# One transfer or four for the first K unit of a decode layer, and four transfers or one for a bias

## The chip, the cores and the metric

The kernel runs on one core of a Trainium2 chip, in one launch. The metric is the device time of that launch in microseconds. The time before is 134.47 us, the median of five runs that lie between 134.28 and 134.51 us.

## The reference

Two tokens (B = 2, one position each, D = 576) go through a layer norm, and then through two branches whose results are added to the input. Branch A is attention against a cache, over the last W = 2048 of 8192 positions; 32 query heads share 16 K/V heads of 128 numbers. Branch B is an MLP with a squared ReLU. Everything in memory is bf16.

```python
xn = layernorm(x)                                  # x: (2, 1, 576)
q  = (xn @ wq).reshape(2, 1, 32, 128)              # wq: (576, 4096)
k  = repeat(k_cache[:, :, 6144:8192, :], 2)        # k_cache, v_cache: (2, 16, 8192, 128)
v  = repeat(v_cache[:, :, 6144:8192, :], 2)
p  = softmax(q . k / sqrt(128))
a  = (p . v) @ wo                                  # wo: (4096, 576)
h  = relu(xn @ w1 + b1) ** 2                       # w1: (576, 4608)
out = x + a + h @ w2 + b2                          # w2: (4608, 576)
```

What has to be read is the last quarter of both caches (33.6 MB) and the four weight matrices (20.1 MB).

## The kernel before

The attention is cut into NU = 8 units. Unit u holds TH = 4 K/V heads of one of the two tokens: 4 x 2048 positions x 128 numbers, 2 MB of K and 2 MB of V. In the tile of a unit, partition p = 4 c + h holds 64 consecutive positions (chunk c of 32) of head h, that is one contiguous row of 16 KB. `unit_view` makes that view of the cache, `issue_kv` takes a buffer and returns the calls that load it, `load_k` and `load_v` call them. K and V units share a pool of six buffers (`kvpool`), which the second MLP matrix uses too at the end.

For each unit `transposes` turns K on TensorE into kT in PSUM (four 128x128 fp32 transposes for each of eight groups), ScalarE and VectorE copy kT to SBUF in turn, `scores` multiplies it with the queries, `softmax` follows, and two units later `pv` multiplies with V. The queries come from `q_block`, which runs after the transposes of unit 0 and needs wq in two transfers: `wq_rem` (0.5 MB) and `wq_big` (4 MB). The MLP's first matrix w1 comes behind the attention's K units, and then the second, w2, whose last rows end the kernel: mlp_o, one copy to `fin_sb` and one transfer out.

All large transfers are issued by SyncE (SP in the profile) in program order: K 0, wq_rem, wq_big, K 1, V 0, K 2, V 1, K 3, V 2, and so on. ScalarE issues the small ones: x at the very start (`xb_sb`, 2 rows), some rows of w2 in five transfers (`w2x_sb`: four of 5 rows of 9 KB, on every fourth partition, and one of 96 rows of 1 KB), the MLP's first bias b1 (`b1_sb`, 4 partitions of 2304 bytes) and the second bias b2 (into row 2 of `xb_sb`).

A planner fixes the order on each engine when the program is built, and places an instruction as early as its operands allow; so the small transfers of ScalarE do not stand where the source has them. It also gives each transfer, SP's and ScalarE's in one common order, one of eight completion semaphores in turn. A transfer that takes a semaphore again waits on its issuing engine until the previous transfer on that semaphore has landed. In the program before the common order begins: x (semaphore 0), K 0 (1), first w2x (2), wq_rem (3), wq_big (4), second w2x (5), b1 in four transfers (6, 7, 0, 1), b2 (2), K 1 (3), V 0 (4), K 2 (5), third w2x (6), V 1 (7), fourth w2x (0), K 3 (1), V 2 (2). So K 1 waits for wq_rem, V 0 for wq_big, K 2 for the second w2x, V 1 and K 3 for two of the b1 transfers, V 2 for b2 and for the buffer of K 0.

Of the kernel before, what the change touches and what calls it, by code (L numbers as in the profile page):

```python
# [9 lines left out]
BF16 = mybir.dt.bfloat16  # L10
# [6 lines left out]
def kernel(  # L17
# [14 lines left out]
    nc = tc.nc  # L32
    P = 128
# [10 lines left out]
    TH = 4  # L44
# [7 lines left out]
    UE = NJ * Dh  # L52
# [13 lines left out]
    NG4 = 4  # L66
# [28 lines left out]
    kvpool = ctx.enter_context(tc.tile_pool(name="kvpool", bufs=6))  # L95
# [17 lines left out]
    k_tiles, v_tiles, wq_tiles, w1_tiles, wo_tiles, w2_tiles = {}, {}, {}, {}, {}, {}  # L113
# [3 lines left out]
    def unit_view(cache, u):  # L117
        tq, b = divmod(u, B)
        return cache[b, tq * TH:(tq + 1) * TH, S0:Sk, :].rearrange("h (c j) d -> c h (j d)", c=CP)

    def issue_kv(tiles, cache, u, name, parts=1):
        tl = kvpool.tile([P, UE], BF16, tag="kv", name=f"{name}_{u}")
        v = unit_view(cache, u)
        n = UE // parts
        tiles[u] = tl
        return [lambda i=i: nc.sync.dma_start(out=tl[:, i * n:(i + 1) * n], in_=v[:, :, i * n:(i + 1) * n])
                for i in range(parts)]
# [62 lines left out]
    nc.vector.memset(eps_t[:], 1e-5)  # L190
    warm = const.tile([B, 2], F32, name="warm")
    nc.scalar.activation(out=warm[:, 0:1], in_=eps_t[:], func=ACT.Sqrt)
    for f in issue_kv(k_tiles, A_k_cache, 0, "k"):
        f()
    NW = 2
    for i in range(NW):
        issue_wq(i)
# [43 lines left out]
    for sg in range(S):  # L241
# [12 lines left out]
                          in_=own[:].unsqueeze(2).to_broadcast([P, NC, HQ // NC]))  # L254
# [275 lines left out]
    load_v(2)  # L530
    b1_sb = const.tile([NG4, HW], BF16, name="b1_sb")
    b1_rows = B_b1.rearrange("(g n) -> g n", g=NG4)
    for i in range(0, NG4, NG4 // 4):
        nc.scalar.dma_start(out=b1_sb[i:i + NG4 // 4, :], in_=b1_rows[i:i + NG4 // 4, :])
    sel4 = const.tile([NG4, P], BF16, name="sel4")
    nc.vector.tensor_copy(out=sel4[:].rearrange("p (g s) -> p g s", s=32),
                          in_=ident[0:NG4, 0:NG4].unsqueeze(2).to_broadcast([NG4, NG4, 32]))
# [67 lines left out]
```

## Time and profile before

| | before |
|---|---|
| median of five runs | 134.47 us |
| the profiled execution | 134.28 us |
| its span | 132.5 us |
| mean granted TensorE clock | 0.834 |
| bytes moved by DMA | 53.76 MB, mean 406 GB/s over the span |
| busy: PE, PEld, DVE, ACT, POOL | 65%, 40%, 43%, 35%, 4% of the span |
| K 0: issued, first transpose that reads it | 0.72 us, 8.45 us |
| wq_rem landed (K 1 is issued) | 9.71 us |
| wq_big landed (V 0 is issued, `q_block` starts) | 19.65 us |
| b1 and b2 issued by ScalarE | 14.40 to 15.82 us |
| last matmul of w2, last copy, transfer out issued | 129.36 us, 129.64 us, 129.95 us |

The span runs from the first to the last event of the profiled execution; the run's time is 1.78 us longer than the span. Busy shares are shares of the whole span, so an engine with 65% can still be the one that is waited for in one stage and idle in another. The DMA share of a stretch is the mean over 16 DMA engines of the time that their packets took; a packet counts where it starts, so a short stretch can show more than 1 and the next one less. In the page's list of DMA queues, q1 carries what SP issues and q10 what ScalarE issues.

### The profile page before, as it was taken

The numbers are of one execution on the slowest core, as the hardware profiler recorded it, in microseconds if no ns is written. First come the engines' busy times: TensorE is split into PE (matmuls) and PEld (weight loads), VectorE is DVE, ScalarE is ACT, GpSimd is POOL, SyncE is SP. The second block draws the span as 40 slices with busy tenths as digits, with TensorE's granted clock in tenths as the row PEclk, the third lists the DMA queues.
The fourth block names the chain that finished last, engine by engine and source line by source line (L and its number), as shares of the span: only waits on it lengthen the run. The fifth ranks groups of instructions, "written<-read, shape, count | busy, mean of one in ns | idle before, by whom it ended". The sixth has DMA issues, their size and how long they took to land.

```text
span 132.5 us, 2337 instructions
## 1 busy us (share of the span) xinstructions
PE 85.5 (65%) x982; PEld 53.0 (40%) x982; DVE 57.2 (43%) x156; ACT 46.6 (35%) x64; POOL 5.2 (4%) x17
## 2 busy tenths in 40 slices
PE   0069509599597679397399689778600938655941
PEld 0058403266364436264256346445400424404930
DVE  6724400525477466476336759456320043344000
ACT  5715500418773375176235346376100040000000
POOL 6000000010010000100100010010100000000000
PEclk9999955958999999999757999999995595555595
DMA  4999999999999999999999999999999999999960
GB/s 154 395 448 456 415 402 427 435 425 435 429 423 424 445 411 424 431 440 420 423 425 445 425 440 433 435 430 444 467 406 388 440 411 444 414 417 444 410 245 1
DMA packets 4219, 53.76 MB, mean 406 GB/s; under 512 B 503, under 2 KB 730, under 8 KB 1246
## 3 DMA queue, kind: packets, MB, share of 16 engines
q1 hardware_dynamic: 4032, 53.32, 94.7%
q10 hardware_dynamic: 178, 0.31, 0.6%
q8 instruction: 7, 0.11, 0.3%
q14 instruction: 2, 0.02, 0.0%
HBM read 53.62 MB, written 0.00 MB: 405 GB/s over the span
## 4 chain that ended last, share of the span: by engine, by line
DMA 61%; PE 6%; DVE 1%; ACT 1%; issue 1%; ACTq 0%
DMA v<-in_A_v_cache_dram 28%; DMA w<-in_B_w_dram 17%; DMA k<-in_A_k_cache_dram 16%; PE kT_ps L108 4%; PE o_ps L105 1%; ACT kT L325 1%; PE sc_ps L105 1%; ACT p L357 1%; DVE pT L360 1%; DVE kT L327 0%; DVE o L386 0%; ACT fin_sb L573 0%; PE out_ps L105 0%; DVE o L384 0%; PE op_ps L105 0%
## 5 line engine op out<-in xcount | busy, mean ns | idle before, releaser
L108 PE MATMUL kT_ps<-ident_f,k 128*128 128x128 f32 x256 | 41.2, 309 | 8.8 <-DMA k<-in_A_k_cache_dram 5.2
L108 PEld LDWEIGHTS kT_ps<-ident_f,k 128*128 128x128 f32 x256 | 32.3, 158 | 22.6 <-issue 10.4
L325 ACT COPY kT<-kT_ps 128x1024 bf16<-128x1024 bf16 x32 | 31.9, 1012 | 22.7 <-PE kT_ps L108 18.4
L327 DVE COPY kT<-kT_ps 128x1024 bf16<-128x1024 bf16 x32 | 21.8, 683 | 13.8 <-PE kT_ps L108 13.5
L105 PE MATMUL sc_ps<-kT,qz 128*32 128x512 bf16 x128 | 10.1, 398 | 6.4 <-DVE kT L327 5.0
L105 PE MATMUL o_ps<-v,pT 128*32 128x512 bf16 x128 | 12.1, 475 | 0.0
L357 ACT ACTIVATE p<-sc_ps,bias 128x512 bf16<-128x512 f32 x8 | 5.5, 688 | 17.6 <-DVE gown L353 17.6
L105 PEld LDWEIGHTS <-xnT 128*2 128x2 bf16 x100 | 3.1, 114 | 16.8 <-issue 16.5
L346 DVE TENSOR_REDUCE m<-sc_ps 128x1 f32<-128x512 f32 x8 | 5.5, 692 | 6.9 <-PE sc_ps L105 6.9
L386 DVE SCALAR_TENSOR_TENSOR o<-o_ps,in_s,o 128x128 f32<-128x128 f32 x24 | 8.3, 347 | 0.5
L360 DVE STREAM_TRANSPOSE pT<-p 128x512 bf16<-128x512 bf16 x8 | 5.7, 712 | 6.5 <-ACT p L357 6.5
L105 PE MATMUL h_ps<-w_big,xnT 128*2 128x384 bf16 x48 | 3.7, 492 | 7.2 <-DMA w_big<-in_B_w_dram 7.2
L573 ACT CAST fin_sb<-out_ps 113x144 bf16<-113x144 f32 x1 | 0.3, 279 | 21.7 <-PE out_ps L105 21.7
L105 PE MATMUL q_ps<-wq_big,xnT 128*2 128x512 bf16 x32 | 3.6, 626 | 4.7 <-DMA wq_big<-in_A_wq_dram 4.7
L350 POOL PARTITION_ALL_REDUCE gmax<-m x8 | 2.9, 365 | 89.4 <-DVE m L348 89.4
L384 DVE TENSOR_SCALAR o<-o_ps,in_s 128x128 f32<-128x128 f32 x8 | 2.7, 338 | 8.1 <-PE o_ps L105 8.1
L105 PEld LDWEIGHTS <-qz 128*32 128x32 bf16 x128 | 2.1, 94 | 10.0 <-DVE kT L327 7.5
L105 PE MATMUL op_ps<-o,of_h 128*128 128x129 f32 x16 | 4.0, 334 | 3.2 <-DVE o L386 3.2
L451 DVE TENSOR_TENSOR hrow<-t 98x384 bf16<-98x384 f32 x3 | 1.6, 556 | 10.0 <-ACT t L450 9.8
L105 PEld LDWEIGHTS <-hT_sb 128*17 128x17 bf16 (+2 forms) x172 | 4.3, 117 | 3.1 <-issue 3.1
L105 PE MATMUL out_ps<-w,hT_sb 128*17 128x144 bf16 x136 | 4.1, 279 | 2.0 <-DMA w<-in_B_w_dram 1.9
L450 ACT ACTIVATE t<-h_ps 98x384 f32<-98x384 f32 x3 | 1.4, 489 | 10.3 <-PE h_ps L105 10.0
(74 smaller groups left out, 52.9 us busy)
## 6 DMA issues: line engine op xcount, KB each, us to landing
k<-in_A_k_cache_dram SPq DMA_DIRECT2D x8, 2048.0 KB, 18.1
v<-in_A_v_cache_dram SPq DMA_DIRECT2D x8, 2048.0 KB, 9.9
wo<-in_A_wo_dram SPq DMA_DIRECT2D x2, 2304.0 KB, 27.4
w_big<-in_B_w_dram SPq DMA_DIRECT2D x1, 4608.0 KB
wq_big<-in_A_wq_dram SPq DMA_DIRECT2D x1, 4096.0 KB, 17.6
w<-in_B_w_dram SPq DMA_DIRECT2D x3, 1296.0 KB, 30.9
w_rem<-in_B_w_dram SPq DMA_DIRECT2D x1, 576.0 KB, 28.2
w<-in_B_w_dram SPq DMA_DIRECT2D x1, 576.0 KB, 22.1
```

What stands on the lines that cost most here:

```text
L105: tc.keep_in_program_order(nc.tensor.matmul(*a, **k))
L108: tc.keep_in_program_order(nc.tensor.transpose(*a, **k))
L325: nc.scalar.copy(out=kT, in_=kT_ps[:])
L327: nc.vector.tensor_copy(out=kT, in_=kT_ps[:])
L346: nc.vector.tensor_reduce(out=m1[:], in_=sc_ps[:], axis=AX.X, op=ALU.max)
L350: nc.gpsimd.partition_all_reduce(gmax[:], m2[:], channels=P, reduce_op=ReduceOp.max)
L357: nc.scalar.activation(out=p_sb[:], in_=sc_ps[:], func=ACT.Exp, bias=bias[:, 0:1], scale=scale, accum_out=o1[:, Dh:Dh + 1])
L360: nc.vector.transpose(out=pT[:].rearrange("p j r -> p (j r)"), in_=p_sb[:])
L384: nc.vector.tensor_scalar(scalar1=in_s[:, 0:1], scalar2=None, op0=ALU.mult, **kw)
L386: nc.vector.scalar_tensor_tensor(scalar=in_s[:, k:k + 1], in1=o1[:, 0:Dh], op0=ALU.mult, op1=ALU.add, **kw)
L450: nc.scalar.activation(out=t1, in_=mlp["ps"][k][0:RB, :], func=ACT.Relu)
L451: nc.vector.tensor_tensor(out=hrow[:, k * HB:(k + 1) * HB], in0=t1, in1=t1, op=ALU.mult)
```

## The change

Two places change. The first K unit is no longer loaded by one transfer of 128 rows of 16 KB, but by four of 32 rows, one for each head: transfer h fills partitions h, h + 4, h + 8, ..., h + 124. The bytes and where they lie in the end are the same. And the bias b1, which came in four transfers of one row, comes in one transfer of four rows.

```diff
-    for f in issue_kv(k_tiles, A_k_cache, 0, "k"):
-        f()
+    k_tiles[0] = kvpool.tile([P, UE], BF16, tag="kv", name="k_0")
+    for h in range(TH):
+        nc.sync.dma_start(out=k_tiles[0][h:P:TH, :], in_=unit_view(A_k_cache, 0)[:, h, :])
...
-    for i in range(0, NG4, NG4 // 4):
-        nc.scalar.dma_start(out=b1_sb[i:i + NG4 // 4, :], in_=b1_rows[i:i + NG4 // 4, :])
+    for i in range(0, NG4, NG4):
+        nc.scalar.dma_start(out=b1_sb[i:i + NG4, :], in_=b1_rows[i:i + NG4, :])
```

The number of transfers stays 40: three more on SP, three fewer on ScalarE. The common order begins differently, though, and with it who waits for whom: x (0), K 0 head 0 (1), first w2x (2), K 0 head 1 (3), second w2x (4), b1 (5), K 0 head 2 (6), b2 (7), K 0 head 3 (0), wq_rem (1), wq_big (2), and from K 1 (3) on as before. On SP, in the order of issue, the transfers now wait like this:

| transfer on SP | waits before for | waits after for |
|---|---|---|
| K 0 | nothing | heads 0 to 2: nothing; head 3: x |
| wq_rem | nothing | K 0 head 0 |
| wq_big | nothing | first w2x |
| K 1 | wq_rem | K 0 head 1 |
| V 0 | wq_big | second w2x |
| K 2 | second w2x | b1 |
| V 1 | second b1 row | b2 |
| K 3 | fourth b1 row | wq_rem |
| V 2 | b2, K 0 transposed | wq_big, K 0 transposed |

ScalarE issues b1 and b2 directly behind the second w2x transfer, before its first copy of kT; before, they stood behind its fourth copy. The first transpose of K 0 waits for four transfers. The order of all other instructions on TensorE, VectorE, ScalarE and GpSimd is unchanged.

## The prediction

> **What bounds the kernel now.** I read four views in this order: busy time by stage, the timeline of the first ten microseconds, SP's waits, and fine stretches around the first packets. The stage view has the length of a stretch, five engines' busy time, the TensorE clock, the DMA share and GB/s.
>
> ```profile
> 0.00:2.00 2.00, 0.00 (x0) 0.00 (x0) 1.07 (x9) 0.68 (x1) 1.47 (x8) 1.00 0.00 1
> 2.00:30.00 28.00, 15.86 (x112) 10.22 (x113) 10.12 (x34) 10.21 (x16) 1.20 (x3) 0.83 1.01 426
> 30.00:60.00 30.00, 23.38 (x221) 14.52 (x219) 18.38 (x43) 17.28 (x24) 1.10 (x3) 0.99 1.01 427
> 60.00:90.00 30.00, 23.53 (x201) 14.16 (x200) 17.49 (x43) 14.29 (x19) 1.09 (x3) 0.89 1.00 428
> 90.00:126.00 36.00, 21.06 (x388) 13.01 (x388) 10.19 (x30) 3.87 (x7) 0.36 (x1) 0.67 1.00 428
> 126.00:129.40 3.40, 1.52 (x64) 1.06 (x63) 0.00 (x0) 0.00 (x0) 0.00 (x0) 0.98 0.59 229
> ```
>
> From 2 to 126 us the DMA share is 1.00 at 426 to 428 GB/s in every stage, while no compute engine is full. So the DMA engines set the end: time is the moment when they start, plus bytes over rate, plus a fixed tail (last bytes of w2, 0.27 us of matmul, 0.28 us of copy, the transfer out). A change counts if it moves the start of the feed, lets the feed run dry, lowers its rate or adds packets. When a transfer is issued, or K 0 transposed, does not count while others are queued.
>
> The timeline (start, duration, what) shows how the feed begins.
>
> ```profile
> 0.72 0.61 SPq L126 DMA_DIRECT2D k<-in_A_k_cache_dram  x1
> 0.73 0.56 ACTq L188 DMA_DIRECT2D xb_sb<-in_A_x_dram  x1
> 1.39 0.57 SPq L138 DMA_DIRECT2D wq_rem<-in_A_wq_dram  x1
> 1.44 0.80 ACTq L184 DMA_DIRECT2D w2x_sb<-in_B_w_dram  x1
> 2.00 0.42 SPq L132 DMA_DIRECT2D wq_big<-in_A_wq_dram  x1
> 8.45 5.79 PE L108 MATMUL kT_ps<-ident_f,k 128*128 128x128 f32 x27 [1.32 <-DMA k<-in_A_k_cache_dram]
> 9.71 0.56 SPq L126 DMA_DIRECT2D k<-in_A_k_cache_dram  x1
> ```
>
> SP's waits show the semaphores at work: K 1 stands 7.3 us until wq_rem has landed, V 0 9.4 us until wq_big has.
>
> ```profile
> SPq L126 <- DMA wq_big<-in_A_wq_dram: 9.4, 1, 9.4
> SPq L126 <- DMA wq_rem<-in_A_wq_dram: 7.3, 1, 7.3
> ```
>
> Stretches of 0.1 us show when the first packets start: x at 1.6 to 1.7, K 0 from 2.1 on.
>
> ```profile
> 1.60:1.70 0.10, 0.00 (x0) 0.00 (x0) 0.10 (x2) 0.10 (x1) 0.10 (x2) 1.00 0.07 23
> 2.00:2.10 0.10, 0.00 (x0) 0.00 (x0) 0.10 (x1) 0.10 (x1) 0.10 (x1) 1.00 0.00 0
> 2.10:2.20 0.10, 0.00 (x0) 0.00 (x0) 0.10 (x1) 0.10 (x1) 0.10 (x2) 1.00 4.92 1311
> 2.20:2.30 0.10, 0.00 (x0) 0.00 (x0) 0.10 (x2) 0.10 (x1) 0.10 (x1) 1.00 1.71 492
> 2.30:2.40 0.10, 0.00 (x0) 0.00 (x0) 0.10 (x2) 0.10 (x1) 0.10 (x1) 1.00 2.25 655
> 2.40:2.50 0.10, 0.00 (x0) 0.00 (x0) 0.09 (x2) 0.10 (x1) 0.10 (x1) 1.00 0.57 164
> ```
>
> **Part 1, the feed starts earlier.** A row of 16 KB starting within 0.1 us counts as 164 GB/s, so 8, 3, 4 and 1 packets start in the last four stretches, one for each DMA engine, at 2.24 us in the mean: 1.52 us after the issue at 0.72. x, with 2 rows, needed 0.92 us (0.73 to 1.65). A quarter has 32 rows. If it took as long as 128 rows nothing is gained; if as long as 2 rows, 0.60 us. A straight line between the two rows gives 0.92 + 0.60 x 30/126 = 1.06 us, a gain of 0.46. SP's issue itself hardly follows the rows (w2x of 96 rows took 0.32 us, one row of b1 0.25), so I take a little less: -0.40 us, bounds 0 and -0.60.
>
> **Part 2, three more transfers.** Each adds a completion on up to 16 engines, 48 small packets. q10's 178 packets take 0.6% of 16 x 132.5 us, 12.7 us; its 0.31 MB take 11.7 us at the 26.6 GB/s per engine of q1 (53.32 MB in 94.7%). The rest is 6 ns a packet: 48 x 6 ns / 16 = +0.02 us, bounds 0 and 0.05.
>
> Whether a transfer of its own has a fixed cost that the queue doesn't hide shows in wq_rem: 0.52 MB behind K 0, it landed 9.71 - 8.45 = 1.26 us after it, which is 416 GB/s and leaves no room for one. [...]
>
> **Part 3, new waits on SP.** Behind each stands every later transfer on SP.
> - Head 3 waits for x, which VectorE reads at 2.93. First bytes by 2.93 + 1.52 = 4.45; heads 0 to 2 (1.57 MB at 426 GB/s, 3.7 us from 1.84) last to 5.5. Nothing.
> - wq_rem waits for head 0: 1.84 + 1.23 us of bytes + 0.4 (the first packets are slow: all 16 of them start before 2.5, none between 2.5 and 3.0) + 0.4 to the landing = 3.9, first bytes 5.4; K 0 lasts to 7.2. Nothing.
> - wq_big waits for the first w2x. Before, its five rows start between 5.5 and 6.5, behind K 0's first rows, and its five completions between 6.5 and 7.5, so it landed near 7.5. wq_rem's bytes ran out on the engines between 8.5 and 9.3, say 8.9; with Part 1, 8.5. If w2x moves with the feed it lands at 7.1 and wq_big's bytes come at 8.6, 0.1 late; if it is served sooner, since fewer rows stand ahead of it, nothing is late; if it stays at 7.5, 0.5 is lost. I take +0.05, bounds 0 and 0.5; the rival below goes further.
> - K 1, V 0, K 2, V 1, K 3 and V 2 wait for small or earlier transfers. They were issued from 9.71 to 24.13 behind wq_big's 9.9 us of bytes with the share at 1.01; earlier issue gains nothing, and the later order of waits is unchanged.
>
> **Part 4, b1 and ScalarE.** Three issues of 0.24 to 0.26 us leave ScalarE at 14.4 to 15.8, where it idles 8.6 us until 24.03: 0. b1 and b2 are now issued near 5.3, ahead of its first copy at 9.60, in its 3.68 us of idle time; without that cover they would delay kT copies by 0.5 us, and PE waits until 19.67 for wq_big anyway. Bytes of b1 stay equal; should one engine have carried all four rows and end last, 6.9 KB / 26.6 GB/s = 0.26 us go. No row shows that; I take 0.
>
> **Part 5, TensorE.** The first transpose waits for four landings instead of one. They come by about 8.1; the work behind it has 4.7 us of slack before wq_big. 0.
>
> **Sum.** -0.40 + 0.02 + 0.05 = -0.33 us. The profiled run took 134.28 us (span 132.5, 1.78 around it), 0.19 under the median; its span would be 132.17. Against the median: 134.47 - 0.33 = **134.14 us**.
>
> **Rivals.**
> - *The start doesn't move*, or the new wait gives it back: 134.47 + 0.02, and 134.4 to 134.6 with half the bounds. For it: SP's issue does not shrink with rows (0.33 to 0.61 for 128). Against it: x's first packets, issued together with K 0's, start 0.44 us before K 0's earliest.
> - *The feed runs dry before wq_big* (slower). SP's three further issues hold back ScalarE's w2x issue, which already took 0.80 us beside SP's against 0.68 later. If it comes 1.2 us later, it lands at 8.7, wq_big's bytes come at 10.2 instead of 8.5: 134.14 - 0.05 + 1.7 = 135.8. It decides from a landing of w2x after 7.7 us (then 0.6 is lost against 0.33 won). The far end: the w2x of 96 rows landed 8.2 us after its issue; 1.44 + 8.2 = 9.6, 2.6 us lost, 136.7. Against it: w2x has fewer rows ahead of it.
> - *Quarters move slower than whole loads* (slower): the slowest stretch of the feed, 2.5 to 5.5, moved 344 GB/s. K 0's 2.10 MB at that rate take 6.1 instead of 4.9 us: 135.3. Against it: in the 5 us behind the third and fourth w2x issue, whose rows lie on every fourth partition too, the rate is 442 GB/s.
>
> [...]
>
> **How the numbers follow.** 0.2% is 0.27 us, about what a measurement of this kernel can tell from no change. Forecast 0.64 (own range 133.85 to 134.4; 0.46 faster, 0.17 same, 0.01 slower); start unmoved 0.14 (0.01, 0.11, 0.02); feed dry 0.14 (0, 0.02, 0.12); quarters slower 0.08 (0, 0.01, 0.07). Sum: faster 0.47, same 0.31, slower 0.22. Range 133.8 (start at its bound, with some of b1's 0.26) to 135.0, which takes in the milder half of the dry feed.
>
> **What would show it.** Right: first K 0 packets between 1.6 and 2.0, the first transpose near 8.1, q_block near 19.3, the share 1.0 from 2 to 126, the last copy near 129.3. Wrong: first packets at 2.1 again; a hole in the DMA share between 7.5 and 10; the first transpose after 8.6 with packets longer than now. A time above 135.0 means a dry feed or slow quarters; one below 133.8 that something else ended last.

## The result

| | before | after |
|---|---|---|
| median time | 134.40 us (48 executions) | 135.22 us (27 executions, 134.76 to 137.18) |
| ratio to before | 1 | 1.0059, 95% interval 1.0046 to 1.0072 |
| span of the profiled execution | 132.5 us | 133.2 us |
| mean granted TensorE clock | 0.834 | 0.839 |

Ratios compare undisturbed executions only, medians are over all, so the two can differ a little. The change makes the kernel slower, by 0.8 us (0.6%). That is outside the range of the prediction, 133.8 to 135.0, and on the other side of it.

### The profile page after: what moved, and what is told of

Read it like the earlier page. It is cut to its first block, busy times and chain, and to the rows that moved or that the text cites. A ratio compares the mean times of both kernels' runs of the same rounds, so it can differ in the third digit from the quotient of the medians.

```text
span 133.2 us, 2340 instructions
## 1 busy us (share of the span) xinstructions
PE 84.9 (64%) x982; PEld 52.9 (40%) x982; DVE 57.0 (43%) x156; ACT 46.5 (35%) x64; POOL 5.2 (4%) x17
## 3 DMA queue, kind: packets, MB, share of 16 engines
q1 hardware_dynamic: 4080, 53.32, 94.7%
## 4 chain that ended last, share of the span: by engine, by line
DMA 76%; PE 14%; SPq 2%; issue 2%; DVE 1%; ACT 1%; ACTq 0%; DVEq 0%
DMA w_big<-in_B_w_dram 28%; DMA k<-in_A_k_cache_dram 17%; DMA w<-in_B_w_dram 17%; DMA wq_big<-in_A_wq_dram 11%; PE kT_ps L108 5%; PE h_ps L105 3%; DMA w2x_sb<-in_B_w_dram 3%; PE q_ps L105 3%; PE sc_ps L105 1%; SPq L138 1%; DVE qrow L292 1%; PE o_ps L105 1%; ACT kT L326 1%; DVE qz L308 0%; SPq L157 0%
## 5 line engine op out<-in xcount | busy, mean ns | idle before, releaser
L108 PE MATMUL kT_ps<-ident_f,k 128*128 128x128 f32 x256 | 40.0, 304 | 10.1 <-DMA k<-in_A_k_cache_dram 8.3
```

What stands on the lines that cost most here:

```text
L108: tc.keep_in_program_order(nc.tensor.transpose(*a, **k))
```

## The profile after: where the time went

The busy time by stage has the columns of the stage view above; the last two numbers are the DMA share and GB/s. First the kernel before, with the stages cut at 9.4 us:

```profile
2.00:9.40 7.40, 1.46 (x11) 1.36 (x12) 4.62 (x23) 3.87 (x6) 0.84 (x2) 1.00 1.09 433
9.40:30.00 20.60, 14.40 (x103) 8.85 (x102) 5.50 (x11) 6.34 (x10) 0.37 (x1) 0.76 0.98 423
```

and the changed kernel:

```profile
2.00:9.40 7.40, 0.51 (x6) 0.41 (x6) 4.61 (x23) 3.85 (x6) 0.83 (x2) 1.00 0.95 337
9.40:30.00 20.60, 14.44 (x109) 9.93 (x109) 5.64 (x12) 6.19 (x10) 0.17 (x1) 0.83 1.02 437
30.00:60.00 30.00, 23.43 (x212) 14.24 (x211) 17.42 (x42) 17.33 (x23) 1.29 (x4) 0.94 1.01 428
60.00:90.00 30.00, 23.45 (x213) 14.03 (x215) 18.48 (x47) 14.57 (x19) 1.09 (x3) 0.94 1.01 430
90.00:126.00 36.00, 20.15 (x359) 12.18 (x362) 9.73 (x28) 3.55 (x7) 0.36 (x1) 0.65 1.00 428
```

From 2.0 to 9.4 us the rate is 96 GB/s lower: 0.71 MB less have been started. Since a packet counts whole where it starts, some of that returns in the next stages (14 GB/s over 20.6 us, 1 and 2 GB/s over 30 us each: 0.38 MB). What is left, 0.33 MB at 427 GB/s, is 0.78 us. The transfer out is issued at 130.70 us instead of 129.95, 0.75 us later. So the whole loss arises before 9.4 us; from there on the feed runs at its old rate, and nothing else ended last.

The timeline of the changed kernel (start, duration, what) shows what SP and ScalarE issued, and the first transpose:

```profile
0.72 2.48 SPq L195 DMA_DIRECT2D k<-in_A_k_cache_dram  x4
...
4.33 0.34 SPq L138 DMA_DIRECT2D wq_rem<-in_A_wq_dram  x1
4.62 0.68 ACTq L184 DMA_DIRECT2D w2x_sb<-in_B_w_dram  x1
5.34 0.48 ACTq L535 DMA_DIRECT2D b_sb<-in_B_b_dram  x1
5.75 0.33 SPq L132 DMA_DIRECT2D wq_big<-in_A_wq_dram  x1
...
9.65 6.46 PE L108 MATMUL kT_ps<-ident_f,k 128*128 128x128 f32 x32 [2.54 <-DMA k<-in_A_k_cache_dram]
...
130.70 0.63 ACTq L575 DMA_DIRECT2D out_dram<-fin_sb  x1
```

A quarter of K 0 takes SP as long to issue as the whole did: four in 2.48 us, begun at 0.72, 1.32, 1.95 and 2.58, against 0.61 us for one. The first transpose comes 1.2 us later than before (8.45), `q_block` at 20.70 instead of 19.65; neither is on the path.

Stretches of 0.1 us around the first packets of K 0, after:

```profile
2.00:2.10 0.10, 0.00 (x0) 0.00 (x0) 0.10 (x1) 0.10 (x1) 0.10 (x1) 1.00 2.57 655
2.10:2.20 0.10, 0.00 (x0) 0.00 (x0) 0.10 (x1) 0.10 (x1) 0.10 (x2) 1.00 3.32 983
2.20:2.30 0.10, 0.00 (x0) 0.00 (x0) 0.10 (x2) 0.10 (x1) 0.10 (x1) 1.00 1.42 492
2.30:2.40 0.10, 0.00 (x0) 0.00 (x0) 0.10 (x2) 0.10 (x1) 0.10 (x1) 1.00 1.71 492
```

At 164 GB/s a row these are 4, 6, 3 and 3 rows, 2.18 us in the mean against 2.24 before. A transfer of 32 rows starts no sooner than one of 128.

The loss itself shows in stretches of half a microsecond. Before:

```profile
4.50:5.00 0.50, 0.00 (x0) 0.00 (x0) 0.50 (x6) 0.50 (x1) 0.00 (x0) 1.00 1.14 426
5.00:5.50 0.50, 0.00 (x0) 0.00 (x0) 0.18 (x2) 0.50 (x1) 0.00 (x0) 1.00 0.53 229
5.50:6.00 0.50, 0.00 (x0) 0.00 (x0) 0.04 (x1) 0.41 (x2) 0.00 (x0) 1.00 1.38 565
6.00:6.50 0.50, 0.00 (x0) 0.00 (x0) 0.46 (x2) 0.00 (x0) 0.00 (x0) 1.00 0.59 248
```

and after:

```profile
4.50:5.00 0.50, 0.00 (x0) 0.00 (x0) 0.50 (x6) 0.50 (x1) 0.00 (x0) 1.00 0.51 197
5.00:5.50 0.50, 0.00 (x0) 0.00 (x0) 0.17 (x2) 0.50 (x1) 0.00 (x0) 1.00 2.62 551
5.50:6.00 0.50, 0.00 (x0) 0.00 (x0) 0.06 (x1) 0.40 (x2) 0.00 (x0) 1.00 0.23 98
6.00:6.50 0.50, 0.00 (x0) 0.00 (x0) 0.46 (x2) 0.00 (x0) 0.00 (x0) 1.00 0.46 197
```

In the stretch from 5.0 to 5.5 the changed kernel starts 551 GB/s x 0.5 us = 0.28 MB, that is fourteen rows of 16 KB and five of w2x's rows of 9 KB. The fourteen take 19 us of the 2.62 x 16 engines x 0.5 us = 21 us of engine time: 1.4 us a row. Before, from 4.5 to 5.0, thirteen rows take 9.1 us, 0.70 each. Afterwards, until 6.5, few rows start. By 5.0 us two quarters (1.05 MB, 2.5 us of feed from 2.2 us on) have been moved: the rows that stall are mostly those of the **third quarter**. They start on time, 3.1 us and more after their issue, and take long; that such a long row is waiting for the rest of its transfer is an inference, no view shows what a row waits for.

## First experiments: which part, and what about it

**b1 alone.** K 0 whole as before, b1 in one transfer.

```diff
-    for h in range(TH):
-        nc.sync.dma_start(out=k_tiles[0][h:P:TH, :], in_=unit_view(A_k_cache, 0)[:, h, :])
+    for f in issue_kv(k_tiles, A_k_cache, 0, "k"):
+        f()
```

> Only the bias part of the change: K 0 in one transfer as before, b1 in one transfer. If the whole loss of 0.8 us lies in the four transfers of K 0, this is within 0.2 us of before (134.2 to 134.6), the DMA share from 2.0 to 9.4 us stays at 433 GB/s and the first transpose stays at 8.4 us. If b1 and b2, issued near 5.3 us instead of 14.4, disturb the start, the feed between 5 and 7 us drops under 400 GB/s here too and the time is 134.7 to 135.2.

Measured: 134.63 us, ratio 1.0018 (1.0009 to 1.0027), 0.12 to 0.36 us more than before; 2.0 to 9.4 us at 428 GB/s, 9.4 to 30 at 423 as before. So K 0's split has the larger part of the loss, 1.0059 / 1.0018 = 0.4% or 0.55 us, and b1 some 0.24 us. One thing the edit doesn't keep: in this kernel the planner puts b1 at 13.99 us, close to its old place, and not at 5.34 as in the changed kernel. The early place of b1 is in the row halves further below, with the same 134.63 us.

**Column quarters.** K 0 in four transfers of 128 rows of 4 KB.

```diff
-    for h in range(TH):
-        nc.sync.dma_start(out=k_tiles[0][h:P:TH, :], in_=unit_view(A_k_cache, 0)[:, h, :])
+    for f in issue_kv(k_tiles, A_k_cache, 0, "k", parts=4):
+        f()
```

> K 0 still in four transfers of 0.5 MB issued one after the other at the start, but each over all 128 partitions with a quarter of every row (4 KB), so all four heads are in each; b1 in one transfer. Theory 'supply': at an empty queue four transfers reach the DMA engines too slowly one after the other, so the feed runs dry between them whatever their shape: 2.0 to 9.4 us at some 340 GB/s, first transpose after 9.3, 135.0 to 135.4 us. Rival 'one head at a time': reading one head's 0.5 MB on all engines at once is slow, and mixing the heads cures it: 425 GB/s or more, first transpose by 8.6, 134.2 to 134.6 us.

Measured: 135.24 us, 1.0069 (1.0056 to 1.0082), 2.0 to 9.4 us at 370 GB/s. The loss doesn't come from the 32 rows or the partitions h, h + 4, ...

**Another unit, in mid-stream.** The kernel before, with K 3 split by heads instead of K 0.

```diff
+        if u == 3:
+            k_tiles[u] = kvpool.tile([P, UE], BF16, tag="kv", name=f"k_{u}")
+            for h in range(TH):
+                nc.sync.dma_start(out=k_tiles[u][h:P:TH, :], in_=unit_view(A_k_cache, u)[:, h, :])
```

> The kernel before, K 0 and b1 as they were; K 3 is loaded by heads in four transfers instead, when the queue has several MB ahead of it. 'Supply': no loss, 134.2 to 134.6 us, and the stretch in which K 3 moves (about 35 to 45 us) stays at 425 to 430 GB/s. 'One head at a time': K 3 moves like K 0 after the change, 1 us or more longer, and the time is 135.0 to 135.4 us.

Measured: 134.61 us, 1.0031 (1.0012 to 1.0050); 9.4 to 30 us at 422 GB/s and 30 to 60 at 428, as before. Quarters of that shape move at full rate behind a full queue. The kernel is nevertheless 0.2 us slower by the medians (0.4 by the ratio), just outside what was expected and clear of the noise, with a feed that shows no loss. This is not located, and since b1 is unchanged here, it warns against laying a loss of 0.2 us to b1.

**Another order of heads.** `for h in (2, 3, 0, 1)`.

> The changed kernel with the heads of K 0 in the order 2, 3, 0, 1. 'Supply': the slow stretch stays at the third transfer's place, near 5.0 to 6.5 us at 100 to 200 GB/s, and the time is as in the changed kernel (135.0 to 135.4). If the rows of head 2 are slow in themselves, the slow stretch moves to 2.5 to 4 us.

Measured: 135.26 us, 1.0084 (1.0053 to 1.0116). The slow rows stay where the third quarter stands, though it is now head 0's: from 5.0 to 5.5 us 518 GB/s start at a share of 2.11, among them 13 rows of K 0 that take 1.2 us each. So it isn't one head's address.

## Second experiments: supply or collision

The theory was now *supply*: at the start the quarters come one by one, and the engines wait for them. Its rival was a *collision* with ScalarE's early transfers.

**Two queues.** Heads 0 and 1 from SP, 2 and 3 from ScalarE.

```diff
-        nc.sync.dma_start(out=k_tiles[0][h:P:TH, :], in_=unit_view(A_k_cache, 0)[:, h, :])
+        (nc.sync if h < 2 else nc.scalar).dma_start(out=k_tiles[0][h:P:TH, :], in_=unit_view(A_k_cache, 0)[:, h, :])
```

> The changed kernel with heads 0 and 1 of K 0 issued by SP and heads 2 and 3 by ScalarE, so that the four quarters are handed over in about half the time. Supply (the quarters come one by one into an empty queue, 0.6 us of issuing apiece, and the DMA engines stand between them): most of the 0.6 us goes, 134.6 to 134.9 us, 2.0 to 9.4 us at 390 GB/s or more (337 in the changed kernel, 433 before). Collision (the stretch at 5 to 7 us is slow because ScalarE's transfers or something else at that time meets K 0's, whoever issues it): 135.1 to 135.4, below 370 GB/s.

Measured: 134.95 us, 1.0030 (1.0014 to 1.0047), 2.0 to 9.4 us at 405 GB/s. As supply expects, if a little slower: half of the loss goes. (The 405 GB/s are from the profiled execution, which took 135.78 us.)

**w2x later.** `issue_w2x` called two steps later (`u >= 5` for `u >= 3`, `u >= 3` for `u >= 1`).

> The changed kernel with ScalarE's first two w2x transfers (issued at 1.43 and 4.62) put off by two steps, so that b1 and b2 alone lie beside K 0. Supply: nothing gained, 135.1 to 135.4, 2.0 to 9.4 us at about 340 to 360 GB/s. Collision with w2x: the loss of the four quarters goes, 134.5 to 134.8, above 410 GB/s; only the quarter of a microsecond that b1's part alone cost stays.

Measured: 135.58 us, ratio 1.0069 (1.0049 to 1.0090), which is 135.3 against 134.39. Nothing gained: w2x is not the cause.

**Two halves.** `issue_kv(..., parts=2)`: 128 rows of 8 KB, twice.

> The changed kernel with K 0 in two column halves (128 rows of 8 KB each) in place of four quarters. Supply, with a price for each transfer that joins an almost empty queue: one of three additional transfers stays, 134.63 (b1's part alone) + 0.6 / 3 = 134.8, bounds 134.7 and 135.0; 2.0 to 9.4 us near 410 GB/s. A loss that depends on any splitting at all, or on a collision at a given time: 135.1 to 135.4, below 380 GB/s.

Measured: 134.68 us, 1.0023 (1.0014 to 1.0031), 421 GB/s. That is b1's part alone; one cut of K 0 costs nothing.

**wq_big first.** `issue_wq(1)` ahead of the four quarters, `issue_wq(0)` behind them.

> The changed kernel with wq_big (4.2 MB in 128 rows) ahead of the four quarters of K 0, and wq_rem behind them, so that the quarters join a full queue at once after the start. Supply: the loss of the quarters goes, 134.4 to 134.8, 2.0 to 9.4 us above 420 GB/s. If quarters are slow at the start wherever they stand, or something else at 5 to 7 us slows all transfers: 135.1 or more and below 390 GB/s. TensorE starts later, which costs nothing as long as the DMA share stays at 1.0 to the end.

Measured: 135.14 us, 1.0053 (1.0041 to 1.0065), so neither of the two as written. The trace shows where: the fourth quarter takes wq_big's turn of the semaphores and waits 10.7 us for it. Timeline of SP, then three stretches:

```profile
13.97 0.47 SPq L196 DMA_DIRECT2D k<-in_A_k_cache_dram  x1
14.48 0.58 SPq L138 DMA_DIRECT2D wq_rem<-in_A_wq_dram  x1
```

```profile
15.00:17.00 2.00, 0.00 (x0) 0.00 (x0) 0.00 (x0) 0.00 (x0) 0.00 (x0) 1.00 1.05 426
17.00:18.20 1.20, 0.00 (x0) 0.00 (x0) 0.00 (x0) 0.00 (x0) 0.00 (x0) 1.00 0.50 154
18.20:20.00 1.80, 1.26 (x6) 1.29 (x7) 0.00 (x0) 0.13 (x1) 0.00 (x0) 1.00 1.10 416
```

The quarters run at 426 GB/s, but wq_rem, issued at 14.48 and wanted near 17, leaves a hole: half of the feed is missing from 17.0 to 18.2. A transfer issued 2.5 us before its turn came too late. That was the first sign of the delay that the last runs measure. The fourth quarter just ahead of it, issued at 13.97 with the engines as full, was not late: the feed shows no hole before 17.0, and by the bytes moved (0.52 MB at 426 GB/s, ending there) its rows start between 15.8 and 16.9 us, right behind the third's, 1.8 to 3 us after the issue; that is an estimate.

This run holds a second finding. With wq_big first, the feed starts earlier:

```profile
1.70:1.80 0.10, 0.00 (x0) 0.00 (x0) 0.07 (x1) 0.10 (x1) 0.10 (x1) 1.00 6.45 1638
```

Its first rows come 1.0 us after the issue at 0.72, where K 0's came 1.4 to 1.7 us after it, though wq_big too has 128 rows.

## Third experiments: when a transfer comes, and two tries for a faster version

**A large part first.** K 0 in columns of 14, 1 and 1 KB a row.

```diff
-    for h in range(TH):
-        nc.sync.dma_start(out=k_tiles[0][h:P:TH, :], in_=unit_view(A_k_cache, 0)[:, h, :])
+    for a, z in ((0, 7168), (7168, 7680), (7680, UE)):
+        nc.sync.dma_start(out=k_tiles[0][:, a:z], in_=unit_view(A_k_cache, 0)[:, :, a:z])
```

> The changed kernel with K 0 in three column parts of 14, 1 and 1 KB a row (128 rows each). Supply (the third transfer of SP's queue reaches the DMA engines only 4 to 5 us after the start, however early it was issued; that shows as a stall only if the first two run out before): the first part alone lasts to about 6.5 us, so nothing is lost, 134.5 to 134.8 us, 2.0 to 9.4 us at 415 GB/s or more. A price for each further transfer at the start, wherever its bytes stand, or something that slows the engines from 5 to 6.5 us once K 0 is cut in three or more: 134.95 to 135.3, 390 GB/s or less.

Measured: 134.91 us, 1.0036 (1.0023 to 1.0049), 376 GB/s. Between the two: 0.3 us more than b1 alone, lost while the first part still ran. This was not explained.

**Small parts first.** The same with `((0, 512), (512, 1024), (1024, UE))`.

> The changed kernel with K 0 in three column parts of 1, 1 and 14 KB a row. Supply, as above: the first two parts (0.26 MB) are gone 0.6 us after the start, and the engines stand until the third comes, at 5 to 6.5 us: 1.5 to 3 us lost, 136.1 to 137.6 us, a hole between 3 and 5 us. If the third transfer came as soon after its issue (1.95) as the first did (1.5 us): a hole of some 0.7 us, 135.2 to 135.5. If only the time from 5 to 6.5 us is slow: no hole before 5, 134.8 to 135.3.

Measured: 135.79 us, 1.0114 (1.0080 to 1.0148). Three stretches:

```profile
2.00:2.70 0.70, 0.00 (x0) 0.00 (x0) 0.67 (x4) 0.69 (x2) 0.70 (x2) 1.00 0.50 108
2.70:3.40 0.70, 0.00 (x0) 0.00 (x0) 0.66 (x4) 0.70 (x2) 0.14 (x1) 1.00 0.76 214
3.40:4.10 0.70, 0.00 (x0) 0.00 (x0) 0.70 (x4) 0.70 (x1) 0.00 (x0) 1.00 1.33 364
```

The third transfer, issued at 2.03, starts from 3.4 us on, 1.4 to 2.1 us after its issue. So the theory as written, that the third transfer always comes 4 to 5 us after the start, fell. Into engines with little to do it comes in about the time that the first needs (0.72 to 2.1).

**A small front.** The kernel before with K 0 in columns of 4 and 12 KB, b1 in four transfers.

> The kernel before with K 0 in two column parts of 4 and 12 KB a row; b1 in four transfers as before. It looks for a faster version: before, the first 16 KB packet of each engine took 0.9 to 1.0 us where later ones took 0.61, and the first 4 KB packets of the four column parts 0.19 to 0.42. If a smaller first row brings the engines to their rate sooner and the second part comes in time (it did in both earlier column splits): 134.1 to 134.3. If the slow first packets are a delay by time and not by size: 134.35 to 134.5.

Measured: 134.79 us, 1.0031 (1.0009 to 1.0052): not faster, and a little slower for one cut, unlike the halves; this was not followed further.

**16 rows first.** The kernel before with K 0 in transfers of 16 and 112 whole rows.

```diff
+    for a, z in ((0, 4), (4, CP)):
+        nc.sync.dma_start(out=k_tiles[0][a * TH:z * TH, :], in_=unit_view(A_k_cache, 0)[a:z])
```

> The kernel before with K 0 in two transfers by rows, the first of 16 rows (one for each DMA engine), the second of 112; b1 in four transfers as before. It tests the step of the prediction that failed, that fewer rows start sooner: x's 2 rows started 0.92 us after the issue, 32 and 128 rows both near 1.5. If 16 rows start like 2: first packets near 1.7 and, if the 112 rows come in time, 134.0 to 134.3. If they start like 32: 2.1 to 2.2 as now, 134.4 to 134.6; more than that if the 112 rows come after 2.8, when the first 16 are through.

Measured: 144.24 us, 1.0723 (1.0694 to 1.0752). No start near 1.7 us, and a loss of 10 us that nobody expected; the last section shows it.

## Fourth experiments: the time from issue to first packet

What was left: is it the number of transfers handed over early, or the time between a transfer's issue and its turn?

**wq_rem in four.** K 0 whole; wq_rem in quarters of 32 rows. As many early transfers as in the changed kernel.

```diff
+            rows = wt[NFULL * P:D, :].rearrange("r (s l) -> (r s) l", s=S)
+            n = 4 if name == "wq" else 1
+            for q in range(n):
+                nc.sync.dma_start(out=tl[q:P:n, 0:lrem], in_=rows[q:P:n, :])
```

> The changed kernel with K 0 whole again and wq_rem, the second transfer of SP, in four quarters of 32 rows (every fourth partition). As many transfers are issued in the first 3 us as in the changed kernel, but K 0 keeps the DMA engines supplied until 7.3 us. Number (each transfer handed over in the first microseconds takes time from the engines, whatever it carries): 134.9 to 135.3, rate from 3.5 to 7 us visibly under 400 GB/s. Place (only transfers whose bytes are wanted within some 3 us of their issue are slow): as with b1's part alone, 134.5 to 134.75, rate about 410.

Measured: 134.54 us, 1.0014 (0.9997 to 1.0031); from 5.0 to 5.5 us 524 GB/s start at a share of 1.23, 0.6 us a row, and 2.0 to 9.4 us run at 416. It is not the number.

**Two row halves.** K 0 by heads 0 and 2, then 1 and 3: 64 rows of 16 KB, twice.

> The changed kernel with K 0 in two transfers of 64 whole rows of 16 KB (every second partition) in place of four of 32. If only the number of cuts counts, as with two column halves (134.68): 134.55 to 134.8. If cutting by rows of 16 KB is itself the trouble: 134.95 to 135.3, with packets over 0.9 us between 4.5 and 7 us.

Measured: 134.63 us, 1.0015 (1.0006 to 1.0024), 428 GB/s. As with column halves, nothing lost beyond b1's part.

**wq_rem first.** `issue_wq(0)` ahead of the four quarters.

> The changed kernel with wq_rem (0.52 MB, 128 rows) issued ahead of the four quarters of K 0, so that 1.2 us more of work lies on the engines when the quarters come, while as many transfers are issued early, and the fourth quarter is held until wq_rem has landed. Place: the quarters after the first two are wanted 1.2 us later, so most of the quarters' loss goes, 134.6 to 134.9. Number, or a slow time from 5 to 7 us whatever is moved then: 135.0 to 135.4.

Measured: 134.86 us, 1.0039 (1.0025 to 1.0054), 0.36 us less than the changed kernel. But this is not simply half of the quarters' loss. Two stretches of this run, and the same of the kernel before:

```profile
1.60:4.00 2.40, 0.00 (x0) 0.00 (x0) 2.22 (x12) 2.38 (x3) 1.23 (x4) 1.00 1.04 383
4.00:7.00 3.00, 0.40 (x6) 0.37 (x6) 2.05 (x12) 1.87 (x4) 0.00 (x0) 1.00 0.97 381
```

```profile
1.60:4.00 2.40, 0.00 (x0) 0.00 (x0) 2.22 (x12) 2.38 (x3) 1.24 (x4) 1.00 0.92 329
4.00:7.00 3.00, 0.38 (x6) 0.37 (x6) 2.04 (x12) 1.88 (x4) 0.00 (x0) 1.00 0.94 381
```

The feed starts earlier: wq_rem's first rows come at 1.7 us, 1.0 us after the issue, like wq_big's above, and by 4.0 us the feed is 54 GB/s x 2.4 us = 0.13 MB or 0.3 us ahead. From 4.0 to 7.0 it runs as before, so the third quarter, wanted about a microsecond later, costs nothing that shows. What is lost is lost at the fourth quarter, which waits for wq_rem to land and is issued late; one line of SP's timeline, and three stretches:

```profile
4.03 0.47 SPq L196 DMA_DIRECT2D k<-in_A_k_cache_dram  x1
```

```profile
6.50:7.00 0.50, 0.40 (x6) 0.37 (x6) 0.34 (x3) 0.00 (x0) 0.00 (x0) 1.00 0.94 393
7.00:7.50 0.50, 0.12 (x2) 0.03 (x1) 0.17 (x2) 0.00 (x0) 0.00 (x0) 1.00 0.53 197
7.50:8.00 0.50, 0.00 (x0) 0.00 (x0) 0.48 (x1) 0.00 (x0) 0.00 (x0) 1.00 1.10 393
```

wq_rem and three quarters last to about 7 us. Then the feed halves until the fourth quarter's rows start, from 7.5 us on, 3.5 us and more after the issue at 4.03. The engines were full in between.

So the theory became *delay*: a transfer issued while the engines are full reaches them mostly 3 to 4.5 us after its issue, and one cut costs only what of this its predecessors don't cover. ScalarE's transfers, which have a queue of their own, fit it in the kernel before: the third w2x, issued at 30.94, has no row on the engines before 34.8, the fourth, issued at 38.22, none before 42.1. The fourth quarter of "wq_big first", with 1.8 to 3 us, doesn't fit, so the delay is not one fixed time. Two last kernels keep the number of transfers and the issue times, and change only when the third is wanted.

**64, 32, 32 rows.**

```diff
-    for h in range(TH):
-        nc.sync.dma_start(out=k_tiles[0][h:P:TH, :], in_=unit_view(A_k_cache, 0)[:, h, :])
+    for h, n in ((0, 2), (1, 4), (3, 4)):
+        nc.sync.dma_start(out=k_tiles[0][h:P:n, :], in_=unit_view(A_k_cache, 0)[:, h:TH:n, :])
```

> The changed kernel with K 0 in three transfers of 64, 32 and 32 whole rows. Delay (a transfer issued once the DMA engines are busy reaches them some 4 us after its issue; the first two come sooner): the third, issued near 1.95, comes at 5.6 to 6.4 us and is wanted at about 6.2, so hardly anything is lost: 134.5 to 134.85, 5.0 to 6.0 us at 380 GB/s or more. Count (each further cut costs alike): 134.9 to 135.1, the same as the next kernel.

**32, 32, 64 rows.** The same with `((0, 4), (2, 4), (1, 2))`.

> The changed kernel with K 0 in three transfers of 32, 32 and 64 whole rows: as many transfers and the same issue times as the kernel with 64, 32 and 32. Delay: the third is wanted at 5.0 us and comes at 5.6 to 6.4, as in the changed kernel: 135.0 to 135.35, packets over 1 us that start near 5.0, 5.0 to 6.5 us at 300 GB/s or less. Count: as the kernel with 64, 32 and 32, 134.9 to 135.1.

Measured: 134.58 us, 0.9996 (0.9969 to 1.0022), and 135.43 us, 1.0067 (1.0040 to 1.0094). Two stretches of 64, 32, 32:

```profile
2.00:9.40 7.40, 1.49 (x11) 1.41 (x12) 4.62 (x23) 3.85 (x6) 0.83 (x2) 1.00 1.05 415
5.00:8.00 3.00, 0.51 (x6) 0.40 (x6) 1.69 (x8) 0.90 (x2) 0.00 (x0) 1.00 0.97 398
```

and of 32, 32, 64, whose profiled execution took 135.93 us. By the medians the two are 1.0017 and 1.0080 of the 134.35 measured beside them, whose 23 executions lie between 134.23 and 136.06 us, three of them above 135.4; the ratios are lower.

```profile
2.00:9.40 7.40, 0.51 (x6) 0.40 (x6) 4.62 (x23) 3.86 (x6) 0.83 (x2) 1.00 0.91 324
5.00:8.00 3.00, 0.51 (x6) 0.40 (x6) 1.69 (x8) 0.91 (x2) 0.00 (x0) 1.00 0.91 299
```

From 5 to 8 us, the time of the second half of K 0, the one moves 398 GB/s and the other 299; the kernel before moved 369 there and the changed kernel 321. Three transfers in both, the third issued at 2.02 and at 1.96 us: with the large part first nothing is lost beyond b1's part, with the large part last at least as much as with four quarters. There the engines do stand: from 5.0 to 5.5 us 154 GB/s at a share of 0.59. One price for each cut is ruled out; the delay foretold both, the second 0.1 us too low.

## Why the prediction was wrong, point by point

**Part 1 (start of the feed, -0.40) failed.** It drew a straight line from x's 2 rows (0.92 us to the first packet) to K 0's 128 (1.52). K 0 in 32 rows needed 1.46: a gain of 0.06 us. The bound "nothing" was the right end. The rival "the start doesn't move" had this reading: SP's issue does not shrink with rows (0.61 us for 128, 0.55 to 0.62 for each quarter). The number of rows was the wrong variable: x differs from K 0 in size and issuing engine too, and wq_rem and wq_big, with 128 rows each, started 1.0 us after their issue when they came first. What sets the start is open; SP took 0.37 us to issue either of them, against 0.61 for K 0.

**Part 2 (three more transfers, +0.02) failed in one step, which part 3 shares: the time from issue to first bytes was taken as 1.52 us everywhere**, from the one transfer that started into idle engines. So the further transfers were priced by their completions alone, 48 small packets. Those came as foretold (q1 has 4080 packets instead of 4032), but the split cost 0.55 us. With 1.52 us, the third quarter (issued 1.95) would have had its rows on the engines at 3.5, ahead of its turn at 5.0. The rows that start at 5.0 to 5.5 were through at 5.9 to 7.0 instead of 5.6 to 6.1 (1.4 us a row, some up to 2, where 0.61 is usual). The trace of before held the hint, in the prediction's own words: the first w2x, issued at 1.44, put its rows on the engines between 5.5 and 6.5. It was read as rows standing behind K 0's, not as a delay. The test by wq_rem (416 GB/s, "no room for a fixed cost") was sound for what it tested: a transfer issued 6 us before its turn hides a delay of that length. The quarters of wq_rem (134.54) confirm that, and those in mid-stream as far as their feed goes. It doesn't speak for transfers wanted 3 us after their issue, and the prediction's premise that the time of issue does not count while others are queued holds only as far as these cover the delay. No fixed price for each transfer stands behind the loss either: beside b1's part alone (134.63), two more transfers cost nothing (64, 32, 32 rows: 134.58) or 0.8 us (32, 32, 64: 135.43), by their order alone.

**Part 3, the waits themselves, held.** wq_rem was issued at 4.33 (foretold 3.9), wq_big at 5.75, K 1 at 7.15, and almost nothing behind them was late: the first w2x had landed by 5.75, earlier than the 7.1 of the sum.

**Part 4 (b1, 0) was too small, as far as the runs tell**: the kernel with b1's part alone took 0.12 to 0.36 us more. In the profiled execution its feed moves as many bytes as before up to 126 us, and the transfer out is issued 0.07 us later; the rest is not located. K 3 split in mid-stream, with b1 as before, lost as much, so that b1 is the cause is not shown.

**Part 5 (TensorE, 0) held**: the first transpose came at 9.65 instead of 8.1, and q_block at 20.70, and the DMA share stayed at 1.0 behind them.

**The rivals.** "Quarters move slower than whole loads", priced at 135.3 with a chance of 0.08, had the size almost to the tenth, and by luck: it took a stretch's rate of 344 GB/s for all of K 0. In truth the rows of the second and fourth quarter move at nearly the old pace (0.68 to 0.70 us a row from 3.5 to 4.5 us, 0.63 to 0.65 from 7.0 to 8.0) and mainly the third's take long (1.4). "The feed runs dry before wq_big" named the right kind of loss at the wrong transfer. The sign that it gave, "a time above 135.0 means a dry feed or slow quarters", and the sign "first transpose after 8.6 with packets longer than now" both came true.

What stays open: what in the chip makes the delay under load (no record shows the path between SP's issue and the engines), why it was shorter once (1.8 to 3 us), why the split 14, 1, 1 KB and the small front lose 0.3 us, where b1's 0.24 us lie, and why wq_rem and wq_big start earlier than K 0. No version tried was faster than the kernel before; wq_rem first with K 0 whole behind it, which would keep the earlier start without the quarters, was not tried.

## What to carry to other kernels

At the start of a kernel, and wherever the queue is short, cut a load only so that what is already handed over covers the next part's way to the engines: here 0.9 to 1.7 us after the issue into idle engines, but mostly 3 to 4.5 us once they are full. Two halves of 1 MB passed that test and quarters of 0.5 MB did not. Three parts passed with 64, 32 and 32 rows; those of 14, 1 and 1 KB a row, with the large part first too, lost 0.3 us. When a trace shows how long a transfer takes to start, ask whether the engines were idle or full at that moment, and use the row that has the same state as the transfer to be priced.

## What the runs showed of the hardware that was not expected

The kernel with 16 rows first ran at half rate or less until 18 us:

```profile
2.00:6.00 4.00, 0.00 (x0) 0.00 (x0) 3.15 (x18) 3.87 (x6) 0.84 (x2) 1.00 0.65 167
6.00:12.00 6.00, 0.52 (x6) 0.41 (x6) 1.48 (x6) 0.00 (x0) 0.00 (x0) 1.00 1.04 210
12.00:18.00 6.00, 0.00 (x0) 0.00 (x0) 0.00 (x0) 0.00 (x0) 0.00 (x0) 1.00 0.98 203
18.00:24.00 6.00, 5.48 (x26) 5.51 (x27) 1.48 (x3) 2.97 (x3) 0.00 (x0) 1.00 1.03 446
```

From 6 to 18 us the engines are busy (share 0.98 to 1.04) at 203 to 210 GB/s, half of the 426 that the kernel before reaches from 2 to 30 us, and from 18 to 24 us the rate is 446 again. The 16 rows were meant to go one to each engine, but only four start from 2.0 to 2.5 us (131 GB/s over half a microsecond) and none from 2.5 to 3.0; K 0 whole starts 16 rows in the first of these stretches (524 GB/s). The counts of packets point the same way. In the changed kernel three more transfers bring 48 more packets on q1 with the same rows, 16 each. Here one more transfer brings 2 more (4034 instead of 4032), so the two parts of K 0 have 18 such packets between them where K 0 whole has 16. If each stands for one engine that the transfer runs on, as the four starts suggest, 4 engines had the 16 rows and 14 the 112: an estimate from these counts, since no view names the engines of a transfer. Why this load, and the whole loads behind it, then move at half rate was not tried; that it follows the uneven spread is a guess.
